# Batch 0 of an attention and two-MLP kernel with unscaled P, fp32 blocks of P^T stationary, V with a column of ones moving, and its first 256 queries in a stream of their own

## The chip, the cores and the metric

The kernel runs on one core of a Trainium2 chip. The metric is device time in microseconds. TensorE (PE) multiplies, and its weight loads are a row of their own (PEld); VectorE is DVE, ScalarE is ACT, GpSimd is POOL, and SyncE (SP) issues nearly all DMAs. A lower time is better.

## The reference

Attention over 4 batches, 8 heads, 576 positions and head size 64, with a causal mask and a decay bias from the running sum of the positive part of `s`; then an MLP with softplus, then an MLP whose activation is a rational function, both 512 to 2048 to 512 on 2304 tokens:

```python
scores = scale * q @ k.T                      # scale = 1/8
cum = np.cumsum(np.maximum(s, 0.0), axis=-1)
bias = -(cum[:, :, :, None] - cum[:, :, None, :])
scores = np.where(causal, -1e9, scores + np.minimum(bias, 0.0))
attn = np.exp(scores - scores.max(-1, keepdims=True))
attn = attn / (attn.sum(-1, keepdims=True) + 1e-09)
x = (attn @ v).transpose(0, 2, 1, 3).reshape(2304, 512)
h = x @ w_in;  x = (np.maximum(h, 0) + np.log1p(np.exp(-np.abs(h)))) @ w_out
h = x @ w_in2
g = (a0 + a1*h + a2*h**2 + a3*h**3) / (1 + abs(b0)*abs(h) + abs(b1)*h**2 + 1e-6)
out = g @ w_out2
```

The weights arrive as 64-bit floats and are converted on the chip.

## The kernel before

**Split operands.** Most products use the type fp32r. To keep precision, an operand is split into a rounded part (hi) and the rest (lo), and three products hi*hi, hi*lo, lo*hi are summed. The split of a tile is a copy on ACT (hi) and a subtraction on DVE or POOL (lo). In attention, `ht` and `st` hold both parts of q and k; four extra rows of `st` hold the running sum of `s` and ones, so that the scores' product (`scores`, two matmuls) adds the bias too.

**Attention parts.** A head of a batch is cut into parts of query rows: M (queries 0 to 255), B (256 to 383), H (384 to 575), L (M and B together). A part goes through `s1`/`s2` (scores on PE, mask with row minimum on DVE, Exp with row sum on ACT, `1/(sum+1e-9)` in two small DVE instructions, and the scaling of P by it on POOL, line 315), `t1`/`t2` (transposes of P on PE; `evac_pt` copies them out as hi on ACT, line 362, and lo on DVE, line 363), and `pv` (line 418: V stationary, hi and lo side by side in 128 columns; the hi and lo of P^T moving, 256 columns or more each, so that a product holds the V-hi half and the V-lo half in different partitions; a copy on ACT, line 429, and an addition on DVE, line 430, bring the halves together). The result goes into `x_t[b]`, with the model dimension in the partitions, as the first MLP wants it.

**Batch 0's start.** The first eight parts are the M parts of batch 0's heads. They have inputs of their own (`qk0`, `s0`), split by `prep_hi` and `prep_lo` (lines 232 to 238); `make_cum0` makes the running sum of their 256 positions. `make_cum` (lines 189 to 199) makes it for all heads and writes it to `cum_d` in DRAM, from where every later part loads its rows (line 275). Then come a B and an H part for each of the 8 heads, then the parts of batches 1 to 3.

**MLP.** Tokens are tiled as 256, 256 and four times 448 in the first MLP, and six times 384 in the second. A unit is one tile and one block of 128 of the 2048 hidden columns: `stage_a` (lines 670 to 672: 12 products), three elementwise stages, and `stage_b` (lines 706 to 708: 12 products). Units 0 to 7 are tile 0 with the blocks 0 to 7, units 8 to 15 tile 1 with the same blocks, units 16 to 31 both tiles in turn with the blocks 8 to 15; then come the 448-token tiles. Before a block is used, its weights are loaded and converted (`conv1`: line 536 on POOL, 537 on ACT, 538 and 543 on DVE, 547 on ACT, 548 on POOL, for each of the two halves of a block), and the lo part is written to `l_d` in DRAM (line 557).

**What sets the order.** Parts, conversions and units are recorded in one program; a list scheduler, with priorities by `ahead(...)`, then sets the order on each engine, which is fixed before the kernel runs. `stream` is the list of the steps of all parts, software pipelined (step `s1` of one part beside `t1`, `t2` of the part before it and `pv` of the one before that). Its first stretch, up to `marks[0]`, runs with the first 8 conversions ahead of the MLP; behind it, `gap` runs a share of the stream in each unit: the B and H parts of batch 0 within units 0 to 7, the L parts of batch 1 within units 8 to 31. SP issues its DMAs in order: one that waits for data holds up all behind it.

## Time and profile before

| | |
|---|---|
| time, median of 3 runs | 1103.66 us (1101.42 to 1104.06) |
| span of the profiled execution | 1100.2 us |
| PE, PEld busy | 94%, 84% |
| DVE, ACT, POOL busy | 75%, 76%, 44% |
| DMA | 140.53 MB, mean 128 GB/s |

The page gives the profiled execution as its span, from its first instruction to its last; no device time of that same execution stands beside it, so the runs' median serves, 3.5 us above it. Matmuls overlap, and the page models their ends, so the work of PE is better read from start to start of neighbouring matmuls than from its busy share. The words granted clock stand for the share of full speed that the throttle granted.

### The profile page before, as it was taken

Reading aid. Unit: us, or ns where it says so; the run is one execution under the profiler, and the core shown is the slowest. Engines: PE = TensorE matmul, PEld = TensorE weight load, DVE = VectorE, ACT = ScalarE, POOL = GpSimd, SP = SyncE. Lnnn points to the kernel's source line nnn. Section 1 sums busy time; section 2 is a strip of 40 time slices with the busy share of each in tenths; the row PEclk is TensorE's granted clock in tenths of the full one; section 3 lists DMA queues with packets and bytes.
Section 4 is the critical chain, followed back from the end, with each engine's and each line's share of the span. In section 5 each row is a group of like instructions: output and inputs, shape, how many; then the busy total and the mean of one; then the engine's idle time right before and its main releaser. Section 6 shows DMA issues by size and latency. Waiting matters only on the chain.

```text
span 1100.2 us, 17835 instructions
## 1 busy us (share of the span) xinstructions
PE 1030.3 (94%) x5732; PEld 926.5 (84%) x5732; DVE 825.4 (75%) x1904; ACT 836.6 (76%) x1767; POOL 488.2 (44%) x543
## 2 busy tenths in 40 slices
PE   3588889889999999999999999899999999999998
PEld 3477778789888888888999998799999999999996
DVE  6898998777888788886556677667777677776765
ACT  6698888878787788777556555688788888888885
POOL 3655576552222122221244676445445455454543
PEclk9999999999999999999999999899999999999999
DMA  6464566466555464432777974401000010000000
GB/s 227 167 221 158 181 222 217 162 205 178 166 160 158 142 205 132 154 94 66 226 235 223 323 280 149 160 1 45 13 30 29 1 58 1 29 30 1 30 1 29
DMA packets 70493, 140.53 MB, mean 128 GB/s; under 512 B 8384, under 2 KB 23904, under 8 KB 70400
## 3 DMA queue, kind: packets, MB, share of 16 engines
q1 hardware_dynamic: 68000, 135.37, 37.5%
q10 hardware_dynamic: 2400, 4.03, 1.5%
q8 instruction: 45, 0.74, 0.3%
q14 instruction: 48, 0.39, 0.1%
HBM read 112.66 MB, written 22.61 MB: 123 GB/s over the span
## 4 chain that ended last, share of the span: by engine, by line
PE 65%; DVE 5%; DMA 3%; ACT 3%; POOL 2%; issue 2%; SPq 0%; POOLq 0%; ACTq 0%; DVEq 0%
PE h L672 6%; PE h L671 6%; PE h L670 6%; PE acc L715 6%; PE acc L714 6%; PE acc L713 6%; PE at L418 3%; PE at L670 3%; PE at L672 3%; PE at L671 3%; PE acc L706 3%; PE acc L707 3%; PE acc L708 3%; PE at L318 2%; DMA raw64x<-in_w_dram 2%
## 5 line engine op out<-in xcount | busy, mean ns | idle before, releaser
L671 PE MATMUL h<-xs,w1h 128*128 128x448 f32 (+1 forms) x352 | 119.9, 341 | 1.4 <-DVE xs L640 1.4
L670 PE MATMUL h<-xs,w1h 128*128 128x448 f32 (+1 forms) x352 | 119.9, 342 | 1.3 <-DVE e L764 1.0
L707 PE MATMUL acc<-gl,w1h 128*128 128x448 f32 (+1 forms) x352 | 119.1, 338 | 1.2 <-POOL gl L802 1.2
L706 PE MATMUL acc<-gh,w1h 128*128 128x448 f32 (+1 forms) x352 | 119.7, 341 | 0.1
L672 PE MATMUL h<-xs,w1l 128*128 128x448 f32 (+1 forms) x352 | 118.8, 338 | 0.2 <-POOL w1l L548 0.2
L708 PE MATMUL acc<-gh,w1l 128*128 128x448 f32 (+1 forms) x352 | 118.4, 336 | 0.0
L715 PE MATMUL acc<-w2h,gl 128*128 128x512 f32 x288 | 113.8, 395 | 0.4 <-POOL gl L802 0.4
L713 PE MATMUL acc<-w2h,gh 128*128 128x512 f32 x288 | 113.8, 395 | 0.4 <-ACT gh L800 0.4
L714 PE MATMUL acc<-w2l,gh 128*128 128x512 f32 x288 | 113.6, 394 | 0.0
L315 POOL TENSOR_SCALAR PA<-PA,stat 128x384 f32<-128x384 f32 (+3 forms) x112 | 69.3, 622 | 97.2 <-DVE stat L314 51.9
L802 POOL TENSOR_TENSOR gl<-PA,gh 128x384 fp32r<-128x384 f32 x96 | 99.4, 1036 | 6.3 <-issue 4.0
L773 POOL TENSOR_TENSOR tc<-tc,e 128x384 f32<-128x384 f32 x48 | 51.7, 1076 | 102.7 <-ACT tc L771 102.7
L315 POOL TENSOR_SCALAR P<-P,stat 128x576 f32<-128x576 f32 x32 | 26.2, 819 | 143.2 <-DVE stat L313 50.7
L363 DVE TENSOR_TENSOR ptl<-at,pth 128x384 fp32r<-128x384 f32 (+2 forms) x108 | 60.7, 569 | 16.3 <-ACT pth L362 15.1
L312 ACT ACTIVATE PA<-PA,stat 128x384 f32<-128x384 f32 (+3 forms) x112 | 63.9, 571 | 10.3 <-DVE stat L299 9.0
L670 PEld LDWEIGHTS h<-xs,w1h 128*128 128x128 f32 x352 | 67.0, 191 | 5.5 <-DVE e L764 1.7
L671 PEld LDWEIGHTS h<-xs,w1h 128*128 128x128 f32 x352 | 66.8, 190 | 5.0 <-DVE xs L640 2.2
L707 PEld LDWEIGHTS acc<-gl,w1h 128*128 128x128 f32 x352 | 66.4, 189 | 4.9 <-POOL gl L802 2.0
L362 ACT ACTIVATE pth<-at 128x384 fp32r<-128x384 f32 (+2 forms) x108 | 53.3, 499 | 21.4 <-PE at L392 12.2
L706 PEld LDWEIGHTS acc<-gh,w1h 128*128 128x128 f32 x352 | 66.4, 189 | 3.6 <-DVE yb L736 0.5
L672 PEld LDWEIGHTS h<-xs,w1l 128*128 128x128 f32 x352 | 66.6, 189 | 3.1 <-POOL w1l L548 0.4
L708 PEld LDWEIGHTS acc<-gh,w1l 128*128 128x128 f32 x352 | 66.2, 188 | 3.0
(225 smaller groups left out, 3311.9 us busy)
## 6 DMA issues: line engine op xcount, KB each, us to landing
w1l<-l_d SPq DMA_DIRECT2D x148, 256.0 KB
raw<-in_w_dram SPq DMA_DIRECT2D x48, 512.0 KB
raw<-in_qk_dram SPq DMA_DIRECT2D x32, 384.0 KB
l_d<-w1l SPq DMA_DIRECT2D x32, 256.0 KB
raw64x<-in_w_dram SPq DMA_DIRECT2D x16, 512.0 KB
R<-in_vv_dram SPq DMA_DIRECT2D x16, 320.0 KB
raw<-in_qk_dram SPq DMA_DIRECT2D x8, 576.0 KB
out_dram<-yb SPq DMA_DIRECT2D x18, 256.0 KB
```

What stands on the lines that cost most here:

```text
L312: nc.scalar.activation(pt[:, 0:n], pt[:, 0:n], AF.Exp, bias=mn, scale=-1.0, accum_out=stat[:, i, 1:2])
L315: nc.gpsimd.tensor_scalar(pt[:, 0:n], pt[:, 0:n], stat[:, i, 2:3], 1.0, op0=ALU.mult, op1=ALU.mult)
L670: nc.tensor.matmul(h, wh[:, cs], xh, start=(k == 0), stop=False)
L671: nc.tensor.matmul(h, wh[:, cs], xl, start=False, stop=False)
L672: nc.tensor.matmul(h, wl[:, cs], xh, start=False, stop=(k == KD - 1))
L706: nc.tensor.matmul(o, wh[:, cs], gh, start=first and not both, stop=False)
L707: nc.tensor.matmul(o, wh[:, cs], gl, start=False, stop=False)
L708: nc.tensor.matmul(o, wl[:, cs], gh, start=False, stop=last and (not both or m % 2 == 1))
L713: nc.tensor.matmul(acc[m], gh[:, cs], wh, start=first, stop=False)
L714: nc.tensor.matmul(acc[m], gh[:, cs], wl, start=False, stop=False)
L715: nc.tensor.matmul(acc[m], gl[:, cs], wh, start=False, stop=last)
L802: eng.tensor_tensor(gl, g, f(gh), op=ALU.subtract)
```

## The change

For batch 0 alone (`turned`), and nothing else in the attention:

- P is not scaled. The Exp has no row sum, and the two small instructions and POOL's scaling go. V has a column of ones between the two heads of a pair (129 columns, input `vt`), so the product with V gives the row sums as a 65th column.
- In `pv_turned`, blocks of P^T (128 keys x 128 queries, plain fp32) are stationary and 65 columns of V move. P^T is copied out once, without a split: on ACT in `t1`, on DVE in `t2`. V isn't split. The output has queries in the partitions: one DVE pair for the reciprocal of each part's sums and a multiplication into `x_t[0]`, now laid out with 128 queries in the partitions.
- Batch 0's rows of x must then be transposed for the MLP: in `split_x_` PE transposes them into PSUM, and the split reads from there.
- The scores of the M parts are one plain fp32 product of 66 rows; the first block of queries takes 128 keys instead of 256. `prep_hi`, `prep_lo` and the splits of the running sum go. `qk0` is loaded with 64 partitions instead of 128.
- The eight M parts are a stream of their own, `steps(0, N0)`, drained before the B and H parts start; `turn0` splits tile 0's x in it, after each pair of heads. In it, the 8 conversions start after a third of its steps instead of half, `make_cum` is placed at that third instead of ahead of the stream, and the conversions' temporary comes from the larger pool `xs`. `load_raw` is now called in that stream too, for six M parts and three pairs of V, whose tiles nothing reads.

Places in the diff:

```diff
+        if p.turned:
+            nc.scalar.activation(pt[:, 0:n], pt[:, 0:n], AF.Exp, bias=mn, scale=-1.0)
+            return
         nc.scalar.activation(pt[:, 0:n], pt[:, 0:n], AF.Exp, bias=mn, scale=-1.0, accum_out=stat[:, i, 1:2])
...
     def scores(o, p, q0, k0, n):
+        if p.first:
+            nc.tensor.matmul(o, p.ht[:, 0, q0:q0 + 128], p.ht[:, 1, k0:k0 + n], start=True, stop=True)
+            return
...
+            n = 128 if p.first else 256
+            scores(bk[:, 0:n], p, 0, 0, n)
+            scores(bk[:, n:n + 256], p, 128, 0, 256)
...
+        if p.turned:
+            c0 = 0 if n == 3 else 320
+            nc.scalar.activation(p.pt[:, c0:c0 + n * 128], bk[:, 0:n * 128], AF.Copy)
...
+            if p.turned:
+                nc.vector.tensor_copy(p.pt[:, 384:768], bk[:, 0:384])
...
+        if p.turned:
+            nc.vector.tensor_copy(p.pt[:, 0:320], bk[:, 64:384])
...
+    def pv_turned(p):
+        bk = abank()
+        hd = p.h % 2
+        lo = [[(0, 0)], [(0, 128), (1, 256)]]
+        hi = [[(c, 384 + c * 128) for c in range(3)]]
+        far = [[(c, 320 + c * 128) for c in range(4)], [(c, c * 64) for c in range(5)]]
+        q0, blocks = {"M": (0, lo), "L": (0, lo + hi), "B": (2, hi), "H": (3, far)}[p.kind]
+        nb = len(blocks)
+        w = D + 1
+        for j, ops in enumerate(blocks):
+            for i, (c, o) in enumerate(ops):
+                nc.tensor.matmul(
+                    bk[:, j * w:(j + 1) * w], p.pt[:, o:o + 128], p.vs[:, c, hd * D:hd * D + w],
+                    start=(i == 0), stop=(i == len(ops) - 1))
...
+        nc.vector.tensor_scalar(rs[:, :, 1:2], o[:, :, D - hd * D:D - hd * D + 1], 1.0e-9, None, op0=ALU.add)
+        nc.vector.reciprocal(rs[:, :, 2:3], rs[:, :, 1:2])
+        for j0, j1, qb, m in ((0, 1, 3, 128), (1, 2, 0, 64)) if p.kind == "H" else ((0, nb, q0, 128),):
+            nc.vector.tensor_tensor(
+                x_t[p.b][0:m, qb:qb + j1 - j0, p.h * D:(p.h + 1) * D], o[0:m, j0:j1, hd:hd + D],
+                rs[0:m, j0:j1, 2:3].broadcast_to([m, j1 - j0, D]), op=ALU.mult)
...
+    steps(0, N0)
+    marks.append(len(stream))
+    steps(N0, NP_)
...
-        n_c = n_st - n_st // S_START
+        n_c = n_st // 3
...
+            if n == n_c:
+                load_raw(allp[N0])
+                load_raw(allp[N0 + 1])
+                with ahead(P_CUM):
+                    make_cum()
...
+                src = x_t[b][:, k, s0:s0 + w] if b else abank()[:, 0:w]
+                if b == 0:
+                    for q in range(0, w, 128):
+                        m = min(128, w - q)
+                        nc.tensor.transpose(
+                            src[:, q:q + m], x_t[b][0:m, (s0 + q) // 128 % 4, k * 128:(k + 1) * 128], ident[0:m, 0:m])
```

How the order moves, at three places. First PE at its very start. Before, the scores of the first head pair, and the head of PE's order, are pairs of a product on `ht` (128 rows) and one on `st` (68 rows):

```order
L318 MATMUL acc<-ht_135 128x256
L318 MATMUL h<-ht_135 128x256
L319 MATMUL acc<-st_136 128x256
L318 MATMUL acc<-ht_135 128x256
L319 MATMUL acc<-st_136 128x256
L319 MATMUL h<-st_136 128x256
L318 MATMUL h<-ht_135 128x256
L319 MATMUL h<-st_136 128x256
```

Now each query block is one product on the raw tile, the transposes (line 367) follow the fourth, and the products with P^T stationary (line 414) come next:

```order
L300 MATMUL acc<-raw_129 128x128
L300 MATMUL acc<-raw_129 128x256
L300 MATMUL h<-raw_129 128x128
L300 MATMUL h<-raw_129 128x256
L367 MATMUL acc<-ident,gh 128x128 x3
L300 MATMUL at<-raw_131 128x128
L300 MATMUL at<-raw_131 128x256
L367 MATMUL h<-ident,gh 128x128
L414 MATMUL acc<-v_133,pt 128x65 x3
```

Four products of 256 columns for a head became two, of 128 and 256 columns.

Second, DVE around one B and H pair in the stretch of units 0 to 7. Before (lines 313 and 314 are the row sums' reciprocal, 363 the lo parts, 430 the addition, 299, 305 and 308 the masks, 282 and 283 the split of q and k):

```order
L305 ISA P_747,stat<-acc,mask 128x288
L305 ISA stat 128x1
L283 TENSOR_TENSOR ht<-raw,ht 64x576
L313 TENSOR_SCALAR stat<-stat 128x1
L430 TENSOR_TENSOR x_277<-acc,tmp 64x192
L314 RECIPROCAL stat<-stat 128x1
L363 TENSOR_TENSOR ptl<-at,pth 128x384
L308 ISA P_747,stat<-at,mask,stat 128x288
L308 ISA stat 128x1
```

Now (421, 422 and 424 are the reciprocal and the multiplication of `pv_turned`, 386 and 394 the copies of P^T):

```order
L283 ISA P_748,stat<-at,mask 128x288
L283 ISA stat 128x1
L422 RECIPROCAL stat<-stat 128x2
L386 COPY pt<-acc 128x384
L424 TENSOR_TENSOR x_220<-at,stat 128x64
L424 TENSOR_TENSOR x_220<-at,stat 64x64
L286 ISA P_748,stat<-acc,mask,stat 128x288
L286 ISA stat 128x1
L421 TENSOR_SCALAR stat<-at 128x1
```

The reciprocals no longer stand between Exp and the transposes, and the subtraction of the 512-column P^T (line 363) has no successor here: ACT copies that tile alone.

Third, SP's queue around the write of `cum_d`. Before, four weight halves (line 521) are issued ahead of it (line 199), and two of V for later pairs (line 259):

```order
L521 DMA raw_199<-in_w_dram 128x1024
L521 DMA raw_201<-in_w_dram 128x1024
L259 DMA R<-in_vv_dram 128x640 x2
L521 DMA raw_395<-in_w_dram 128x1024
L521 DMA raw_397<-in_w_dram 128x1024
L253 DMA raw<-in_qk_dram 128x896
L199 DMA cum_d<-rows 128x1152
L521 DMA raw_440<-in_w_dram 128x1024
```

Now two halves (line 561) stand ahead of it (line 194), then loads that nothing reads (line 221 with 256 columns, line 228 with 258), and the third and fourth halves stand behind it:

```order
L561 DMA raw_171<-in_w_dram 128x1024
L221 DMA raw<-in_qk_dram 128x2x256
L228 DMA vr<-in_vt_dram 128x258
L221 DMA raw<-in_qk_dram 128x2x256 x2
L228 DMA vr<-in_vt_dram 128x258
L221 DMA raw<-in_qk_dram 128x2x256
L221 DMA raw<-in_qk_dram 128x896
L228 DMA vr<-in_vt_dram 128x645
L194 DMA cum_d<-rows 128x1152
L561 DMA raw_276<-in_w_dram 128x1024
L561 DMA raw_278<-in_w_dram 128x1024
```

Two weight halves moved behind the wait for the running sum, and six loads without a reader stand ahead of it.

## Rows read from the trace of the kernel before

**Rows 1.** Busy time by stretch of the span (us, with instructions)
```profile
core 0: us, PE busy (x) PEld busy (x) DVE busy (x) ACT busy (x) POOL busy (x), PEclk, DMA share, GB/s
...
11.00:57.00 46.00, 25.52 (x96) 20.67 (x95) 36.16 (x115) 31.12 (x78) 26.89 (x34) 1.00 0.63 211
57.00:137.00 80.00, 67.38 (x471) 59.80 (x470) 72.62 (x210) 70.27 (x169) 43.50 (x51) 0.98 0.56 184
137.00:170.00 33.00, 29.02 (x222) 26.90 (x222) 30.89 (x79) 28.22 (x78) 23.05 (x28) 1.00 0.69 231
170.00:240.00 70.00, 59.86 (x471) 57.20 (x470) 53.94 (x131) 57.94 (x149) 45.32 (x53) 1.00 0.57 189
240.00:520.00 280.00, 276.80 (x1648) 243.72 (x1647) 224.43 (x701) 221.17 (x503) 63.52 (x97) 1.00 0.48 146
```
**Rows 2.** Timeline, up to the first mask: start, duration, instruction, idle before it
```profile
2.46 0.46 DVE L166 TENSOR_SCALAR cum<-s_t 32x256 f32<-32x256 f32 x1 [1.30 <-DMA s_t<-in_s_dram]
...
7.44 2.68 SPq L215 DMA_DIRECT2D st<-cumc  x4
...
9.55 0.55 PE L319 MATMUL acc<-st 68*128 68x256 f32 x1 [1.31 <-ACT st L233]
...
11.00 0.29 DVE L299 CUSTOM_DVE_ANT_0 gh<-acc,mask 128x128 f32<-128x128 f32 x1
```
**Rows 3.** DVE by line and shape, 0 to 57 us: busy, mean ns
```profile
L237 DVE TENSOR_TENSOR st<-raw,ht 64x512 fp32r<-64x512 f32 x4 | 3.1, 775 | 2.6 <-ACT ht L232 2.6
L363 DVE TENSOR_TENSOR ptl<-acc,pth 128x384 fp32r<-128x384 f32 x5 | 2.7, 549 | 0.6 <-ACT pth L362 0.5
L314 DVE RECIPROCAL stat<-stat 128x1 f32<-128x1 f32 x18 | 2.7, 156 | 0.1
L313 DVE TENSOR_SCALAR stat<-stat 128x1 f32<-128x1 f32 x18 | 2.6, 146 | 0.3
```
**Rows 4.** PE's timeline, 27 to 57 us
```profile
39.06 0.41 PE L318 MATMUL acc<-ht 128*128 128x256 f32 x1
39.27 0.41 PE L319 MATMUL acc<-st 68*128 68x256 f32 x1
...
48.41 0.66 PE L318 MATMUL at<-ht 128*128 128x384 f32 x1 [1.68 <-ACT raw L537]
...
55.17 0.41 PE L670 MATMUL h<-xs,w1h 128*128 128x256 f32 x1
```
**Rows 5.** SP's timeline, 0 to 75 us
```profile
30.51 0.33 SPq L199 DMA_DIRECT2D cum_d<-rows  x1
...
35.40 3.11 SPq L557 DMA_DIRECT2D l_d<-w1l  x2
...
39.07 0.31 SPq L275 DMA_DIRECT2D st<-cum_d  x1
```
**Rows 6.** DVE by line and shape, 57 to 137 us
```profile
L314 DVE RECIPROCAL stat<-stat 128x1 f32<-128x1 f32 x25 | 3.9, 155 | 0.2
...
L363 DVE TENSOR_TENSOR ptl<-acc,pth 128x512 fp32r<-128x512 f32 x5 | 3.4, 680 | 0.0
...
L291 DVE TENSOR_TENSOR vs<-R,vs 128x640 fp32r<-128x640 f32 x3 | 2.9, 959 | 0.0
```
**Rows 7.** PE's timeline, 57 to 70 us
```profile
64.95 0.77 PE L392 MATMUL at<-ident,P 128*128 128x128 f32 x5 [1.27 <-POOL P L315]
65.47 0.48 PE L318 MATMUL at<-ht 128*128 128x512 f32 x1
...
66.49 0.77 PE L418 MATMUL acc<-pth,vs 128*128 128x256 f32 x5
67.09 0.76 PE L418 MATMUL acc<-ptl,vs 128*128 128x256 f32 x5
```
**Rows 8.** Waits, 57 to 137 us: total, times, longest
```profile
PEld at L392 <- POOL P L315: 5.3, 5, 1.6
```
**Rows 9.** ACT by line and shape, 57 to 137 us
```profile
L312 ACT ACTIVATION_READ_ACCUMULATOR PA<-PA,stat 128x1 f32 x17 | 3.2, 189 | 0.0
```

More of the change, by code (lines that the diff above doesn't have):

```diff
@@ L118, in moe_chain_kernel, with __init__ @@
     class Part:
[L119 removed]
+        def __init__(self, b, h, kind, rng, first, turned):
             self.b, self.h, self.kind, self.rng = b, h, kind, rng
[L121 removed]
+            self.fresh, self.first, self.turned = rng is not None, first, turned
     def cols(t, rng):
@@ L365, in t1 @@
     def t1(p):
-        p.ph, p.pl = pt_h[p.idx % 2], pt_l[p.idx % 2]
+        if p.turned:
+            p.pt = t_j("pt", [128, 1024], F32)
+        else:
+            if not pt_h:
+                for i in range(2):
+                    for lst, nm in ((pt_h, "pth"), (pt_l, "ptl")):
+                        t = t_j(nm, [128, 1024], F32R)
+                        nc.gpsimd.memset(f(t[:, 0:192]), 0.0)
+                        lst.append(t)
+            p.ph, p.pl = pt_h[p.idx % 2], pt_l[p.idx % 2]
         if p.kind == "B":
@@ L369, in t1 @@
         bk = abank()
-        if p.kind in "LM":
-            for i, c0 in enumerate((256, 0, 128)):
-                nc.tensor.transpose(bk[:, i * 128:(i + 1) * 128], p.p1[:, c0:c0 + 128], ident)
+        n = 3 if p.kind in "LM" else 4
+        order = (256, 0, 128) if n == 3 and not p.turned else range(0, n * 128, 128)
+        for i, c0 in enumerate(order):
+            nc.tensor.transpose(bk[:, i * 128:(i + 1) * 128], p.p1[:, c0:c0 + 128], ident)
+        if p.turned:
+            c0 = 0 if n == 3 else 320
+            nc.scalar.activation(p.pt[:, c0:c0 + n * 128], bk[:, 0:n * 128], AF.Copy)
+        elif n == 3:
             evac_pt([t[:, 192:576] for t in (p.ph, p.pl)], bk[:, 0:384])
         else:
-            for c in range(4):
-                nc.tensor.transpose(bk[:, c * 128:(c + 1) * 128], p.p1[:, c * 128:(c + 1) * 128], ident)
             evac_pt(
@@ L463, in moe_chain_kernel, with steps, at, turn0 @@
         ends.append(n)
-    for i in range(NP_ + 2):
-        def at(j):
-            return allp[j] if 0 <= j < NP_ else None
-        a0, a1, a2 = at(i), at(i - 1), at(i - 2)
-        nx, nx2 = at(i + (2 if i < 6 else 1)), at(i + 2)
-        if i == 6:
-            nx = None
-        if nx2 is not None and 8 <= i + 2:
-            stream.append((load_raw, nx2))
-        if a0 is not None:
-            stream.append((s1, a0))
-        if a2 is not None:
-            stream.append((pv, a2))
-        if i - 1 in ends:
-            marks.append(len(stream))
-        if nx is not None:
-            stream.append((prep, nx))
-        if a1 is not None:
-            stream.append((t1, a1))
-            stream.append((t2, a1))
-        if a0 is not None:
-            stream.append((s2, a0))
+    def steps(lo, hi):
+        for i in range(lo, hi + 2):
+            def at(j):
+                return allp[j] if lo <= j < hi else None
+            a0, a1, a2, nx, nx2 = at(i), at(i - 1), at(i - 2), at(i + 1), at(i + 2)
+            if nx2 is not None:
+                stream.append((load_raw, nx2))
+            if a0 is not None:
+                stream.append((s1, a0))
+            if a2 is not None:
+                stream.append((pv, a2))
+                if a2.first and a2.h % 2 == 1:
+                    stream.append((turn0, a2))
+            if i - 1 in ends[1:]:
+                marks.append(len(stream))
+            if nx is not None:
+                stream.append((prep, nx))
+            if a1 is not None:
+                stream.append((t1, a1))
+                stream.append((t2, a1))
+            if a0 is not None:
+                stream.append((s2, a0))
+    def turn0(p):
+        split_x(0, 0, p.h // 2)
+    steps(0, N0)
+    marks.append(len(stream))
+    steps(N0, NP_)
     pos = [0]
@@ L531, in conv_t @@
         hw = r[:, :, 1]
-        t = sb.tile([128, 512], F32, tag="tc", bufs=2, name="tc")
+        lead = m == 0 and region[0] == 0 and not units_open
+        t = t_xs([128, 512], F32) if lead else sb.tile([128, 512], F32, tag="tc", bufs=2, name="tc")
         ti = t.bitcast(I32)
```

205 lines of the change are left out of this document (91 added, 114 removed).

## The prediction, made before the result was known

> **What bounds the kernel now.** I read the stretches of the span first [rows 1]. From 240 us on PE is busy 276.8 of 280 us, and the batches and tiles worked there are not touched by the change; what moves the end is therefore when the kernel gets to that point. From 57 to 137 us, the stretch in which units 0 to 7 run beside the eight B and H pairs of batch 0, DVE is busy 72.6 of 80 us, ACT 70.3 and PE 67.4. PE's share flatters it: in work from start to start it is less. Five transposes of P take 0.52 us, so 0.104 each, and five products of 256 columns with V take 0.60, so 0.12 each [rows 7]. A unit has 24 products of 256 columns, eight units 192, or 23 us; a head's pair has 12 transposes (1.25), scores with 2944 columns in all (1.4 at the same rate) and 16 products with V (1.9), or 4.55, and eight of them 36. That is 59 of 80 us, so DVE sets this stretch. From 11 to 57 us nothing is full: DVE 36.2 of 46 us, PE 25.5 [rows 1], and PE runs at its lower level: two products of 256 columns start 0.21 us apart at 39 us [rows 4] against 0.12 later, which is 1.2 against 2.4 GHz, although the granted clock reads 1.00. The start is a chain: the input of the running sum is used at 2.46 us, its rows go out by DMA at 7.44, the product that needs them starts at 9.55, the first mask at 11.00 [rows 2]. The first unit starts at 55.17, the first scores of a B part at 48.41 [rows 4].
>
> **Term 1, the first mask: 4 us earlier.** Between 2.46 and 7.44 stand six DVE and two ACT instructions, and ACT is split between them and `prep_hi`. Three in a row are left, at about 0.46 us each by the first [rows 2], with their handovers 1.8 us: the DMA goes out at 4.3 us, lands 2.1 later as before, and the first mask starts at about 7.0.
>
> **Term 2, DVE's work.** Up to 57 us the change takes away: the splits of q and k for two pairs after 11 us (four instructions at 0.78, 3.1 us), the lo parts of P^T of eight M parts (8 x 0.55 = 4.4), eight of sixteen reciprocal pairs (8 x 0.30 = 2.4) [rows 3], and two splits of V (at 0.96 each, 1.9 [rows 6]); 11.8 us. From 57 to 137 us: the lo parts of eight 512-column P^T, which ACT now copies alone (8 x 0.68 = 5.4), four splits of V (3.8), and 8 of 24 reciprocal pairs (2.4) [rows 6]; 11.6 us. The copies of 384 and 320 columns take the place of subtractions of the same size, and three multiplications of 64 columns a pair that of two additions: I count them at nothing, with 1 us either way. From 11 to 137 us DVE is busy 108.8 of 126 us, 86% [rows 1]. Without 23.4 us of it, at that share, the two stretches take 99 us instead of 126: 27 us less, and with term 1 the ceiling is 31 us.
>
> **Term 3, what SP's order gives back: 6 us.** A B part needs its rows from `cum_d`. Their load stands in SP's queue behind four writes to `l_d`, of which two wait for the third and fourth weight halves, whose loads now stand behind the write of `cum_d`; that write waits for `make_cum`. The scan now stands behind five heads' masks on DVE. A head needs about 3 us of PE at the lower level (term 4), so it begins at 22 us, and I put the write at 29 us, against 30.51 now [rows 5]. From the write to the load it takes 8.6 us now (30.51 to 39.07, with the two writes to `l_d` held up till 35.40 [rows 5]); a load and conversion more, some 7 us, and the first scores of a B part come at about 45 us, only 3 us earlier than now. Behind the load wait, on SP, the weight halves that follow. Until 45 us DVE has eight M parts (about 1.6 us each by the masks, the pair and the multiplication), the running sum, five or six halves, tile 0's split and one part's split of q and k: some 27 us of the 33 that it would do at 86%. The 6 us are lost, between 0 (if the parts aren't late) and 14 (if the fourth half is one more round late). The loads without a reader are covered by the free half of the DMA time there [rows 1]; if they aren't, it is in that 14. The first unit itself, which needs the M parts and one half, starts at about 37 us.
>
> **Term 4, PE's price for plain fp32: 4 us.** The trace shows plain fp32 only as transposes: 128 columns and a load of a 128x128 fp32 tile, 0.104 us [rows 7]. A product with V now loads such a tile and moves 65 columns. Lower end: a transpose, 0.10. Upper end: four, 0.42. I take 0.20, by the nearest row, the transpose, doubled because a product must carry the digits that a transpose passes through. A pair then has 12 such products, 2.4 us instead of 1.9; PE's work in the stretch becomes 63 us of the 67 that DVE would need, and two engines that full wait for each other: 4 us. At 0.10 it is 53 us and nothing is lost. For the M parts, at the lower level: scores 384 columns, between 0.32 us (the rate of [rows 4]) and four times that; with the upper end, 0.5 for transposes and 3 x 0.4, a head takes 3.0 us, eight heads 24, and the stream ends near 35 us with its last chain. The 20 new transposes of x cost 2 us of PE where it waits anyway.
>
> The Trainium skill bears on this price. FP8 and Floating Point Precision, TensorE Precision Notes, gives true FP32 four passes through the array, and TensorE: Matmul & The Clock Gate, Terms, calls the transpose mode four times faster for FP32. By these the price is the upper end, 0.42, if each pass loads its tile, and about a product of 260 columns, 0.12, if the loads hide; no row here shows which. The first makes rival B.
>
> **Covers.** POOL's scaling goes for batch 0. It held PE five times, 5.3 us in all [rows 8], but off DVE's path, which is late next; I count nothing. ACT loses 25 reads of row sums (0.19 each [rows 9]) and most copies, and is not late. From 137 to 240 us nothing is removed; I pass the gain on whole.
>
> **Sum.** 31 - 6 - 4 = 21 us. The span goes from 1100.2 to 1079; the runs' median lies 3.5 us above the span, so 1103.66 - 21 gives 1083 us. About 0.3%, 3.3 us, is what a measurement of this kernel can tell from no change.
>
> **Rivals.**
>
> A, the forecast, 1083 (1073 to 1092): 58%.
>
> B, PE takes over. At 0.42 us a pair costs PE 7.7 us with transposes and scores, the stretch 23 + 61 = 84 us: no gain there. The M stream takes 4.3 us a head, 34 us, and the B parts start no earlier; of the ceiling 13 us of the second stretch and 11 of the first are gone: 31 - 24 = 7, 1097 us. For it: the rule above. Against it: the products of a group share nothing that must be loaded four times, and the transpose pair already includes its load. 12%.
>
> C, the gain is given back before 240 us. From 170 to 240 us sixteen units take 70 us for 46 us of PE work, and no engine is full (PE 59.9, ACT 57.9 [rows 1]): the conversions run as a chain through POOL, ACT and DVE. If they set their own pace from the start, through SP's order, half of the 21 us is lost there: 1093. Against it: the halves are placed by units, and start earlier with them. 13%.
>
> D, slower. The same place as B at a higher price: at 0.55 us the stretch has 23 + 8 x 9.25 = 97 us of PE work, 17 more than it takes now, and the M stream 5.1 us a head, 41 us, so the first unit starts at 54 and nothing is won ahead of it but some 4 us; 1103.66 + 13 gives 1117. It decides from about 0.47 us a product on. Against it: this is more than four transposes. 8%.
>
> E, more than the sum: terms 3 and 4 are nothing, and DVE's copies and multiplications are shorter than what they replace: 1070. 9%.
>
> **Range and chances.** 1068 to 1100 leaves out D, parts of B and the end of E, some 15%. Faster by more than 0.3% are A, E and most of B and C: 0.84; within 0.3% the upper part of B: 0.08; slower 0.08.
>
> **What would show it.** The first mask near 7 us; the write of `cum_d` near 29, the first scores of a B part near 45, the first unit near 37; the stretch of the eight pairs about 71 us instead of 80, with DVE's work about 11 us less; the distance from its end to the end of the span unchanged within 3 us. PV products 0.2 us apart at the higher level. The forecast is wrong if these products stand 0.4 us apart, if the write of `cum_d` or the third half comes later than now, or if the stretch from the last H part to the 448-token tiles grows.

## The result and the profile after

The changed kernel takes 1110.25 us (median of 4 runs, 1106.57 to 1113.17) against 1103.42: a ratio of 1.007, 95% interval 1.0045 to 1.0094. Run again beside the experiments it gave 1110.75, ratio 1.0063 (1.004 to 1.0085). It is slower, by 0.6 to 0.7%; forecast were 1083 us and a gain of 21. Its two traces are of runs of 1106.57 and 1106.05 us, so a trace of it shows less than it lost: the span is 1104.8 us, 4.6 longer than before (1104.2 in the second trace), where the medians lie 7 to 9 us apart. A run's time is 1.8 us above its own span (1106.57 and 1104.8); the rest of the 3.5 us between median and span before is the distance of the traced run from the median.

Busy time by stretch of the changed kernel, columns as in [rows 1]:
```profile
core 0: us, PE busy (x) PEld busy (x) DVE busy (x) ACT busy (x) POOL busy (x), PEclk, DMA share, GB/s
...
11.00:57.00 46.00, 33.19 (x129) 27.99 (x128) 25.64 (x75) 21.60 (x45) 13.14 (x14) 1.00 0.61 196
57.00:137.00 80.00, 72.48 (x516) 67.45 (x516) 61.80 (x192) 57.77 (x111) 30.43 (x35) 0.97 0.63 203
137.00:170.00 33.00, 30.76 (x238) 29.61 (x237) 29.17 (x82) 29.22 (x80) 23.75 (x27) 0.97 0.67 221
170.00:240.00 70.00, 59.50 (x447) 57.27 (x446) 52.29 (x130) 56.05 (x141) 45.53 (x52) 0.95 0.58 189
240.00:520.00 280.00, 277.31 (x1666) 244.35 (x1666) 223.46 (x696) 221.07 (x504) 66.94 (x99) 1.00 0.49 146
```
DVE lost the work that was to go: 36.2 to 25.6 us from 11 to 57, 72.6 to 61.8 from 57 to 137. PE took its place as the fullest engine: 25.5 to 33.2 and 67.4 to 72.5. From 170 to 240 us the granted clock is 0.95, where before it was 1.00.

The start, against [rows 2, 4]; the first mask, and one M head on PE:
```profile
4.65 2.61 SPq L204 DMA_DIRECT2D raw<-cumc  x4
...
8.67 1.62 PE L300 MATMUL acc<-raw 66*128 66x128 f32 x4 [8.67 <-DMA raw<-cumc]
...
10.45 0.29 DVE L277 CUSTOM_DVE_ANT_0 gh<-acc,mask 128x128 f32<-128x128 f32 x1 [6.60 <-PE acc L300]
```
```profile
12.17 1.49 PE L300 MATMUL at<-raw 66*128 66x128 f32 x4
13.45 0.42 PE L367 MATMUL h<-ident,gh 128*128 128x128 f32 x1
13.66 1.38 PE L414 MATMUL acc<-v,pt 128*128 128x65 f32 x6
14.84 0.74 PE L300 MATMUL acc<-raw 66*128 66x128 f32 x2
```
A head's plain fp32 scores take 1.28 us (12.17 to 13.45), its three products with V 1.18 (13.66 to 14.84). Each plain fp32 product is two instructions, so "x6" is three products. PE is at its lower level here: a transpose takes 0.21 us (13.45 to 13.66), against 0.104 at the higher [rows 7].

SP of the changed kernel, against [rows 5]; L194 writes `cum_d`, L249 loads rows of it, L221 loads q and k, L561 a weight half, L599 writes a low half:
```profile
35.32 0.33 SPq L194 DMA_DIRECT2D cum_d<-rows  x1
35.70 1.38 SPq L561 DMA_DIRECT2D raw<-in_w_dram  x2
...
50.12 2.00 SPq L599 DMA_DIRECT2D l_d<-w1l  x2
52.22 0.38 SPq L561 DMA_DIRECT2D raw<-in_w_dram  x1
52.65 0.34 SPq L249 DMA_DIRECT2D st<-cum_d  x1
...
65.45 2.87 SPq L599 DMA_DIRECT2D l_d<-w1l  x2
68.36 0.43 SPq L221 DMA_DIRECT2D raw<-in_qk_dram  x1
...
69.33 0.34 SPq L249 DMA_DIRECT2D st<-cum_d  x1
```
The write of `cum_d` comes 4.8 us later than before, the first load of its rows 13.6 later, and the second head's q and k wait until 68.36 behind the writes of low halves.

What this does to PE, against [rows 4, 7]:
```profile
42.59 0.41 PE L718 MATMUL h<-xs,w1h 128*128 128x256 f32 x1
...
56.28 0.66 PE L302 MATMUL acc<-ht 128*128 128x384 f32 x1 [4.03 <-DVE ht L257]
...
77.44 2.12 PE L414 MATMUL acc<-vr,pt 128*128 128x65 f32 x18
79.37 0.38 PE L302 MATMUL acc<-ht 128*128 128x288 f32 x1
...
80.07 0.49 PE L384 MATMUL at<-ident,PA 128*128 128x128 f32 x3
```
The first unit starts 12.6 us earlier, the first B scores 7.9 later, the second head's B transposes at 80.07 (68.3 before). At the higher level nine products with V take 1.93 us, 0.21 each.

**The stations of each trace.** Second head: its B transposes; eighth head: its H transposes; unit 32 is the first on 448 tokens. changed_again is the changed kernel unedited, in a second trace. Times in us; the time and ratio are of all runs. The kernel before was run again beside each group of experiments, with medians from 1101.9 to 1103.1 us, so kernels of different groups are compared by their ratios.

| kernel | second head | eighth head | unit 8 | unit 16 | 16 to 32 | 32 to end | time | ratio (interval) |
|---|---|---|---|---|---|---|---|---|
| before | 68.3 | 134.7 | 130.4 | 170.1 | 70.8 | 859.3 | 1103.4 | |
| changed | 80.1 | 129.7 | 137.2 | 170.4 | 74.3 | 860.1 | 1110.3 | 1.007 (1.0045-1.0094) |
| changed_again | 80.0 | 129.7 | 134.9 | 168.6 | 75.7 | 860.0 | 1110.8 | 1.0063 (1.004-1.0085) |
| late_v | 78.5 | 131.6 | 136.7 | 168.9 | 72.2 | 860.4 | 1102.2 | 0.9986 (0.9971-1.0001) |
| second_head | 72.9 | 126.0 | 132.3 | 166.3 | 72.5 | 860.2 | 1100.4 | 0.9985 (0.9968-1.0002) |
| half_first | 79.2 | 128.9 | 136.2 | 169.5 | 73.4 | 860.6 | 1106.7 | 1.0037 (1.0025-1.0049) |
| few_pv | 78.9 | 128.1 | 131.5 | 166.0 | 72.8 | 863.5 | 1098.2 | 0.9969 (0.9953-0.9985) |
| start_order | 75.5 | 124.7 | 129.9 | 163.0 | 75.8 | 863.3 | 1105.3 | 1.0028 (1.0015-1.004) |
| own_stream_all | 66.2 | 130.8 | 135.3 | 169.4 | 74.7 | 860.2 | 1104.5 | 1.0006 (0.9979-1.0034) |
| own_stream_loads | 64.5 | 125.1 | 127.2 | 162.9 | 71.2 | 861.6 | 1099.0 | 0.9974 (0.9959-0.9988) |
| one_stream | 70.0 | 122.8 | 127.9 | 160.5 | 75.1 | 861.7 | 1098.5 | 0.9963 (0.9948-0.9978) |
| sum_first | 69.7 | 122.5 | 127.7 | 160.2 | 74.7 | 860.6 | 1098.2 | 0.9968 (0.9956-0.998) |
| sum_first_few | 69.4 | 119.5 | 121.8 | 157.5 | 71.1 | 862.6 | 1093.9 | 0.9928 (0.9903-0.9952) |
| sum_first_m | 65.2 | 117.9 | 123.1 | 155.7 | 75.4 | 860.2 | 1093.8 | 0.992 (0.9901-0.994) |
| sum_first_split | 69.9 | 123.7 | 124.2 | 160.5 | 74.7 | 861.1 | 1097.8 | 0.9952 (0.9936-0.9969) |
| sum_first_u0 | 67.2 | 118.9 | 124.1 | 157.8 | 76.3 | 862.8 | 1098.0 | 0.9972 (0.9954-0.999) |
| u0_half_first | 67.3 | 119.1 | 124.3 | 158.1 | 72.1 | 862.1 | 1096.1 | 0.9953 (0.9934-0.9972) |
| u0_and_split | 67.2 | 120.1 | 120.6 | 156.6 | 71.7 | 862.9 | 1093.1 | 0.9913 (0.9893-0.9933) |

From before to changed: the second head comes 11.8 us later, the heads after it follow faster (from the second's B transposes to the eighth's 60.4 us before, 43.5 after), and at unit 16 the two stand level. The forecast had 21 us there. Of the 4.6 us lost in the trace, 3.5 come from units 16 to 32. The two traces of the changed kernel differ by 2.3 us at unit 8, 1.8 at unit 16 and 1.4 over units 16 to 32, so such a difference between two traces shows nothing by itself. The column from unit 32 to the end differs by up to 4 us between kernels whose instructions are the same there, so a span alone decides nothing below that. Runs of one kernel can lie apart too, own_stream_all's the most: four took 1098.0 to 1099.1 us at a mean granted clock of 0.992 to 0.995, six 1102.9 to 1109.2 us at 0.975 to 0.986, and its trace is one of the six.

### The profile page after: what moved, and what is told of

Same layout as the page of the kernel before. It is cut to its first block, busy times and chain, and to the rows that moved or that the text cites. A ratio compares the mean times of both kernels' runs of the same rounds, so it can differ in the third digit from the quotient of the medians.

```text
span 1104.8 us, 17814 instructions
## 1 busy us (share of the span) xinstructions
PE 1048.8 (95%) x5832; PEld 948.6 (86%) x5832; DVE 795.4 (72%) x1847; ACT 812.3 (74%) x1672; POOL 463.5 (42%) x504
## 4 chain that ended last, share of the span: by engine, by line
PE 68%; DVE 9%; DMA 6%; issue 6%; ACT 5%; POOL 5%; SPq 1%; POOLq 0%; ACTq 0%; DVEq 0%
PE h L718 6%; PE h L719 6%; PE h L720 6%; PE acc L768 6%; PE acc L767 6%; PE acc L766 6%; PE at L449 3%; PE at L720 3%; PE at L718 3%; PE at L719 3%; PE acc L759 3%; PE acc L760 3%; PE acc L761 3%; DMA raw64x<-in_w_dram 3%; PE at L302 2%
## 5 line engine op out<-in xcount | busy, mean ns | idle before, releaser
L718 PE MATMUL h<-xs,w1h 128*128 128x448 f32 (+1 forms) x352 | 122.7, 349 | 5.4 <-ACT xs L687 2.9
L719 PE MATMUL h<-xs,w1h 128*128 128x448 f32 (+1 forms) x352 | 122.4, 348 | 1.0 <-DVE xs L688 1.0
L720 PE MATMUL h<-xs,w1l 128*128 128x448 f32 (+1 forms) x352 | 121.5, 345 | 1.1 <-POOL w1l L589 1.1
L759 PE MATMUL acc<-gh,w1h 128*128 128x448 f32 (+1 forms) x352 | 120.6, 343 | 0.1
L296 POOL TENSOR_SCALAR PA<-PA,stat 128x128 f32<-128x128 f32 (+3 forms) x96 | 59.1, 618 | 84.4 <-DVE stat L295 46.2
L718 PEld LDWEIGHTS h<-xs,w1h 128*128 128x128 f32 x352 | 69.1, 197 | 10.3 <-DVE e L817 3.5
L296 POOL TENSOR_SCALAR P<-P,stat 128x576 f32<-128x576 f32 x24 | 20.4, 849 | 130.6 <-DVE stat L294 54.5
L719 PEld LDWEIGHTS h<-xs,w1h 128*128 128x128 f32 x352 | 69.4, 197 | 4.6 <-DVE xs L688 1.6
L720 PEld LDWEIGHTS h<-xs,w1l 128*128 128x128 f32 x352 | 69.1, 196 | 4.5 <-POOL w1l L589 1.6
L760 PEld LDWEIGHTS acc<-gl,w1h 128*128 128x128 f32 x352 | 67.2, 191 | 2.9
L768 PEld LDWEIGHTS acc<-w2h,gl 128*128 128x128 f32 x288 | 54.3, 189 | 13.4 <-POOL gl L855 0.8
L348 DVE TENSOR_TENSOR ptl<-at,pth 128x384 fp32r<-128x384 f32 (+1 forms) x95 | 53.6, 571 | 16.6 <-ACT pth L347 15.2
L767 PEld LDWEIGHTS acc<-w2l,gh 128*128 128x128 f32 x288 | 54.3, 188 | 12.2
```

What stands on the lines that cost most here:

```text
L296: nc.gpsimd.tensor_scalar(pt[:, 0:n], pt[:, 0:n], stat[:, i, 2:3], 1.0, op0=ALU.mult, op1=ALU.mult)
L348: nc.vector.tensor_tensor(l, src, f(h), op=ALU.subtract)
L718: nc.tensor.matmul(h, wh[:, cs], xh, start=(k == 0), stop=False)
L719: nc.tensor.matmul(h, wh[:, cs], xl, start=False, stop=False)
L720: nc.tensor.matmul(h, wl[:, cs], xh, start=False, stop=(k == KD - 1))
L759: nc.tensor.matmul(o, wh[:, cs], gh, start=first and not both, stop=False)
```

## Experiments: the start

Theory S: the order of SP's queue makes the heads late. Theory P: PE is the bound once the heads run. Theory G: what is won by 137 us is given back by 240.

**late_v.** Batch 1's V loads wait for the write of `cum_d`:
```
# make_cum, behind its DMA
+        cum_t["w"] = traced()[-1]
# load_raw, behind the load of R from vv
+                    queue_behind({cum_t["w"].engine: cum_t["w"]}, k0)
```


> The changed kernel, with one edit: the loads of batch 1's first two V tiles, which the changed kernel issues at about 3 us ahead of the rows of the running sum, are held behind the write of cum_d. Theory S (the order of SP's queue at the start costs the time): the rows land about 2 us after their issue instead of 4, the first mask starts near 8.3 us instead of 10.45, and the M stream and the write of cum_d come 2 us earlier; of that at most 2 us reach the end, 1108. Theory P (from 80 us PE is the bound with the turned heads) and theory G (whatever is won ahead of 137 us is given back by 240 us) both say that the end does not move: 1110 within 2 us.

The rows went out at 4.18 and the first product started at 7.85: landing still took 3.7 us, the mask came only 0.8 us earlier. The time fell by 8 us all the same, of which the trace shows 1.5 at unit 16 and 2.1 behind it, where the edit touches nothing. At unit 16 the second trace of the changed kernel is as early as late_v's (168.6 and 168.9). The stretch behind it is taken up below.

**second_head.** The second head's loads stand in the start:
```
-                load_raw(allp[N0 + 1])
+                load_raw(allp[N0 + 2])
...
             prep(allp[N0])
+            prep(allp[N0 + 2])
```


> The changed kernel with one edit: the loads of q, k and of the rows of the running sum for the second head's B and H parts are issued in the start, beside the first head's, instead of behind the eight halves that are converted there. Theory S (the heads from the second on take 7 us each whatever they wait for, so the time at which the second begins sets the end of the stretch): its B transposes at 70 us instead of 80.1, the eighth head's H transposes near 121 instead of 129.7, unit 8 near 129 instead of 137.2, the end 5 to 8 us below the changed kernel's. Theory P (PE is the bound): units 4 and 5, which now run in the gap, are pushed behind the heads, the eighth head comes at 127 or later and the end moves by less than 2 us.

This took 10.4 us less than the changed kernel run beside it (1100.38 to 1110.75; between the ratios lie 0.8%, some 9 us). SP of second_head, L251 loading the rows of two heads:
```profile
47.23 0.55 SPq L221 DMA_DIRECT2D raw<-in_qk_dram  x1
53.20 0.68 SPq L251 DMA_DIRECT2D st<-cum_d  x2
```
The second head came at 72.9, the eighth at 126.0, unit 8 4.9 us earlier, although the write of `cum_d` left 3.5 us later than in the changed kernel (38.79). S holds in sign; but unit 4 moved from 72.4 to 83.1, as P said. The trace has 4.1 us of the gain at unit 16 and 1.7 in units 16 to 32 (2.3 and 3.1 against the second trace of the changed kernel); where the rest arises isn't shown.

**start_order.** The sum ahead of the stream, four halves ahead of it, loads without a reader left out, V late:
```
+        with ahead(P_CUM):
+            make_cum()
         for n in range(n_st):
...
-        load1_to(2)
+        load1_to(4)
...
-        if p.fresh:
+        if p.fresh and not p.first:
```


> The changed kernel with four edits, all of them to what stands on SP and ahead of the first unit: the running sum is emitted ahead of the M stream, four weight halves are loaded ahead of it instead of two, the loads that no one reads (q, k and V of the M parts) are left out, and batch 1's V loads wait for the write of cum_d. Theory S: the write of cum_d at 28 us (35.3 in the changed kernel), the first scores of a B part at 46 us (56.3), the second head's B transposes at 70 us (80.1), the end 10 us earlier: 1100. Theory P: the heads from 80 us on take 7 us each on PE as before, so half of it at most is kept: 1105. Theory G: the unit of tile 1 that opens the next stretch still starts near 137 us, the end at 1109.

It took 1105.3 us, short of S. The write of `cum_d` left at 41.8, not 28: the planner had put it behind two writes of low halves.

**own_stream_all.** start_order, with low halves behind the write, `P_CUM = 400`, and the loads of second_head:

> The changed kernel, with its stream of M parts of its own, and all of the start's edits together: the loads that no one reads left out, batch 1's V loads and the writes of low halves behind the write of cum_d, four weight halves ahead of it, the running sum emitted first with its priority raised from 60 to 400, and the loads for two heads (not one) in the start. Theory S: the write of cum_d at 33 us, the first scores of a B part at 45, the second head's B transposes at 58 to 62, the first unit at 36; the eighth head's H transposes 60 us after the second head's start, 119, unit 8 at 122, the end 1090 to 1093. Theory P (from the second head on PE is full, so units that ran in the gap before are pushed behind): unit 8 at 127 as in sum_first and the end at 1098.

It missed both theories: 1104.5 us, unit 8 at 135.3. The write of `cum_d` left at 40.1, not 33. The second head came at 66.2, the third only at 86.2. SP, with L605 the write of low halves and L222 the third head's q and k:
```profile
69.27 2.90 SPq L605 DMA_DIRECT2D l_d<-w1l  x2
72.28 0.77 SPq L222 DMA_DIRECT2D raw<-in_qk_dram  x1
```
The wait had moved one head on.

**own_stream_loads.** All batch-0 heads' loads ahead:
```
-            with ahead(off):
+            with ahead(400 if fn in (load_raw, prep) and g == 1 else off):
```


> own_stream_all with one more edit: the loads and the preparation of every B and H part of batch 0 have the priority 400, so that on SP the loads of the third to sixth head stand among the first eight writes of low halves and not behind them. Theory S (what the own stream loses is the order of the later heads' loads on SP): third head's B transposes at 73 to 76 us instead of 86.2, the following heads 7 us apart, unit 8 at 125, the end 1092 to 1096. Theory P (PE is the bound from the second head on, whichever work it gets): the heads come earlier and the units 4 to 7 as much later, unit 8 at 130 or later, the end 1100 or more.

The third head came at 74.6, unit 8 at 127.2, between S and P, and unit 16 6.6 us earlier than in own_stream_all: in the traces the later heads' place on SP was the own stream's loss. The time is less sure: 1099.0 us, by the ratios 3.5 us less with intervals that overlap, and four of own_stream_all's runs lie as low.

**one_stream.** The changed arithmetic with the order of before:
```
-    steps(0, N0)
-    marks.append(len(stream))
-    steps(N0, NP_)
+    steps(0, NP_)
```
with the sum, weight halves and gate at the start as in the kernel before (`P_CUM = -100`), and the loads of start_order.

> The changed kernel with its batch-0 arithmetic (plain fp32, turned products) but with the order of the kernel before: one stream for M, B and H parts, the running sum ahead of it, the prepared B parts inside the start, weight halves as in the kernel before; the loads that no one reads are left out and batch 1's V loads wait for the write of cum_d. Theory S: the first scores of a B part at 46 us or earlier, two heads ready together, units 0 to 7 end some 10 us earlier than in the kernel before, and the end is 1092. Theory P: the end stays at 1106 or above since the turned heads cost PE more than they save DVE. Theory G: 1103, as the kernel before.

It took 1098.5 us: the new arithmetic in the old order, without the loads that nothing reads and with batch 1's V loads held back as in late_v, is a gain of 4 us. The changed kernel lies 12 us above it, 9.9 of them at unit 16; that is what its order costs, with those loads. The busy time of one_stream:
```profile
57.00:137.00 80.00, 76.41 (x596) 72.72 (x595) 68.03 (x210) 62.89 (x132) 32.63 (x40) 0.97 0.64 208
```
PE is busy 76.4 of 80 us, DVE 68.0: with the heads in time PE, not DVE, is the fullest engine. What its work there is worth is tested next.

## Experiments: PE's price

**few_pv**, on the changed kernel, and **sum_first_few**, on sum_first:
```
+            if p.kind != "M":
+                ops = ops[0:1]
```


> The changed kernel, but the products of P^T with V of batch 0's B and H parts are cut to the first key block of each: 3 products a head pair instead of 12 (its result is that of a part of the keys only). At the 0.21 us of the trace that takes 1.9 us a head, 15 us in all, from PE and nothing from any other engine. Theory P: most of it, 8 to 12 us, shows at the end: 1100. Theory S: heads start as late as before and only their own chain gets shorter, 3 us: 1107. Theory G: no change, 1110.

> sum_first, with the products of P^T with V of batch 0's B and H parts cut to the first key block of each: 3 instead of 12 for a head pair (its result is that of a part of the keys only), which takes 15 us of work from PE. Theory P: with two heads loaded in time PE is the bound from 57 to 131 us (it is busy 76 of 80 us in the neighbouring kernel one_stream), so unit 8 starts 10 us or more earlier, near 117, and the end falls by 8 or more to 1090. Theory S (each head's own chain of loads, split, scores, mask and exponent takes 7 us, and PE's share of it is small): unit 8 moves by 3 us at most, the end by 3, 1095.

Both leave out most of the products, so their results are not the attention's. few_pv gave 12 us (10 to 11 by the ratios), but its heads still come 7.3 us apart and its traced span is only 2.5 us shorter; the trace is of a run of 1104.12 us, with a granted clock of 0.84 from 57 to 137 us. sum_first_few gave 4.3. Its unit 8 came 5.8 us earlier, between P's 10 and S's 3, and its unit 16 2.8; another 3.6 come in units 16 to 32, where the order on SP changed too, which the next part takes up. So 15 us of PE's work are worth 3 to 6 where the heads are in time, and heads 7.4 us apart instead of 7.9 say that PE is not all that sets them. What else does isn't shown.

**sum_first**, one_stream with
```
         nc.sync.dma_start(out=l_d[ff][half], in_=f(l))
+        queue_behind({cum_t["w"].engine: cum_t["w"]}, k0)
```


> one_stream with one more edit: no write of a low half to l_d stands ahead of the write of cum_d on SP. In one_stream the rows were ready at 34 us and the write left at 38.6, behind two such writes. Theory S: the write leaves at 34, the first load of its rows at 41 or 42 instead of 46.6 and the first scores of a B part 4 us earlier, unit 8 near 124 instead of 127.9, the end 2 to 4 us below one_stream's: 1095. Theory G (half or more of what is won by 130 us is lost by 240 us): 1097. If the weight chain and not the rows paces the start of the heads: no change, 1098.5.

Nothing changed, the third of the cases put down: the write left at 33.9, 4.7 us earlier, and the first B transposes stayed at 56.5. The rows' load didn't move with the write, since it still stands behind writes of low halves and a weight half: it left at 46.66, and at 46.65 in one_stream.

**sum_first_m**, M parts without their off-diagonal block:
```
-            scores(bk[:, n:n + 256], p, 128, 0, 256)
+            scores(bk[:, n + d:n + 256], p, 128, d, 256 - d)   # d = 128 for M
```


> sum_first, with the M parts cut to their two diagonal blocks (queries 128 to 255 don't see keys 0 to 127): 256 instead of 384 columns of plain fp32 scores, two transposes instead of three, two products with V instead of three, which at the lower level is 0.43 + 0.2 + 0.39 us a head, 8 us of PE in all, and 0.1 us a head each of DVE and ACT. If PE's plain fp32 products pace the start (DVE and ACT sat waiting for PE from 10 to 30 us): the running sum's scan 3 us and the last M part's products 6 to 8 us earlier, the first scores of a B part and unit 0 some 4 us earlier, the end 2 to 4 us lower, 1095. If the loads and the conversion of the first weight halves pace it: the M parts end earlier but unit 0 and unit 8 don't move, 1098.

The excerpt is one of several places; queries 128 to 255 leave out keys 0 to 127. Unit 0 came at 53.8 (59.0), unit 16 4.6 us earlier, the end 4.4: of the edits to sum_first this one arrived in full. The M parts' work paces the start, and nearly all that was taken is PE's plain fp32 at the lower level (DVE and ACT lost 0.1 us a head); 1 us of PE a head is worth over 4 us of the end.

**sum_first_split** (tile 1's x turned back per pair) and **sum_first_u0** (unit 0 ahead of the first B work):
```
+SP1B = (5, 3, 2, 1)      # for T = 1, in place of SP1
```
```
+                if i == N0:
+                    stream.append((pv, a1))
+                    stream.append((turn0, a1))
```


> sum_first with one more edit: x of tile 1 is turned back and split for a pair of heads as soon as the pair is done (5, 3, 2 and 1 units ahead of unit 8 instead of 2, 1, 1 and 1), where one_stream had six of its eight transposes between 127.6 and 130.9 us. Theory S adds: if those transposes and splits at the end of the stretch hold unit 8, it starts 2 to 4 us earlier and the end is 2 us lower still, 1093; if the last head's own products hold it, no change against sum_first, or 1 us more since the splits now stand among the heads' work.

> sum_first with one more edit: the last M part's product with V and the turning of tile 0's last x stand ahead of the first B and H parts' scores on PE, not behind them; with that, unit 0 stands ahead of the first B part's transposes. In sum_first PE was busy 28.9 of 46 us from 11 to 57 and unit 0 began at 59.0, behind scores that wait for their rows. Theory P (PE's work up to unit 8 is the bound, so what is done in PE's idle time before 57 us is won): unit 0 at 47 to 50, unit 8 3 us earlier, 124.5, the end 1095. Theory S (the heads' own chain): the heads stay where they are, unit 8 at 127.5 and the end at 1098.

Each put unit 8 3.5 us earlier, and neither median moved by more than 0.4. For sum_first_split the lead was gone at unit 16; for sum_first_u0 it was 2.4 us there (157.8 to 160.2) and 0.8 at unit 32.

## Experiments: units 16 to 32

The table's column for units 16 to 32 has two groups: short, 70.8 to 73.4, and long, 74.3 to 76.3. Which one a kernel falls in goes with one place on SP. What stands there, changed kernel and late_v (numbers of buffers left out):
```
changed                          late_v
st<-cum_d                        st<-cum_d
raw<-in_qk   (waits for DVE)     raw<-in_w
raw<-in_w                        l_d<-w1l
raw<-in_w                        raw<-in_qk
```
All nine traces of the long group have the load of q and k ahead of both halves, as on the left; none of the others has. SP there, changed kernel (L249 rows, L221 q and k, L561 weight halves), then late_v (L252, L222, L564):
```profile
179.80 0.66 SPq L249 DMA_DIRECT2D st<-cum_d  x1
183.83 0.34 SPq L221 DMA_DIRECT2D raw<-in_qk_dram  x1
185.27 0.93 SPq L561 DMA_DIRECT2D raw<-in_w_dram  x2
```
```profile
176.37 0.67 SPq L252 DMA_DIRECT2D st<-cum_d  x1
179.31 0.34 SPq L564 DMA_DIRECT2D raw<-in_w_dram  x1
181.29 0.33 SPq L602 DMA_DIRECT2D l_d<-w1l  x1
183.23 0.34 SPq L222 DMA_DIRECT2D raw<-in_qk_dram  x1
```
What the load of q and k waits for in the changed kernel is DVE's split of an earlier q and k (L257, which ends at 183.75), and not PE, as the expectation of half_first has it; from 176 to 190 us:
```profile
SPq L221 <- DVE ht L257: 3.3, 1, 3.3
```
The half goes out 6.0 us later, 3.4 of which are there at the rows already. POOL's next conversion (L577, in late_v L580) starts 6.7 later:
```profile
191.50 0.64 POOL L577 TENSOR_SCALAR tc<-raw 128x512 f32<-128x512 f32 x1 [2.94 <-PE at L303]
```
```profile
184.83 0.64 POOL L580 TENSOR_SCALAR tc<-raw 128x512 f32<-128x512 f32 x1
```
No edit of late_v stands here: the planner lays the whole program out anew, and a DMA moved at 3 us turned this pair at 180.

**half_first** and **u0_half_first**: the changed kernel and sum_first_u0, with that pair turned and every order up to 170 us left alone:
```
+            if fn is load_raw and g == 2 and p.h == 0:
+                queue_behind({cum_t["lw"].engine: cum_t["lw"]}, k0)   # lw: the last weight half's load
```


> The changed kernel with one edit, which leaves every engine's order as it is up to 170 us: the load of q and k for batch 1's first H part, which waits on SP for PE at about 180 us, is put behind the two weight-half loads that stand right behind it. Theory O (this one order on SP costs the stretch of units 16 to 32 some 3 us, and the edits late_v, second_head and few_pv each owed a part of their gain to changing it): units 16 to 32 take 71 to 72.5 us instead of 74.3 and 75.7, the span is 3 us shorter, and the time 3 to 6 us, 1104 to 1107, a ratio of 1.001 to 1.004 to the kernel before. Theory S alone (the start is the whole loss): no change, 1110.5.

> sum_first_u0 with the same edit as half_first. Theory O: sum_first_u0 opened unit 8 3.6 us earlier than sum_first and ended no earlier, since its units 16 to 32 took 76.3 us; with the half's load first they take 71 to 73, and the end is at 1094 to 1095, near u0_and_split's 1093. Without it: 1098.

half_first took 3.9 us less than the changed kernel's 1110.5, in the range given, though the intervals of the ratios overlap a little. Units 16 to 32 did not do what was expected: they fell by 0.9 us only, within what two traces of one kernel differ by, since the halves still left at 184.3. u0_half_first fell by 1.9 us (intervals overlap), units 16 to 32 by 4.2.

A second thing differs, which no run holds fixed: the granted clock. From 170 to 240 us, for sum_first_u0, u0_half_first and half_first (the changed kernel's row stands above):
```profile
170.00:240.00 70.00, 59.80 (x432) 56.62 (x432) 52.01 (x118) 52.77 (x133) 41.67 (x46) 0.95 0.55 177
```
```profile
170.00:240.00 70.00, 60.86 (x458) 57.31 (x457) 53.35 (x130) 56.03 (x141) 45.22 (x47) 1.00 0.57 186
```
```profile
170.00:240.00 70.00, 58.49 (x458) 55.62 (x457) 51.37 (x128) 56.90 (x143) 45.57 (x52) 1.00 0.58 190
```
A mean of 0.95 over 70 us is at most 3.5 us of PE at full speed, an estimate from this row alone, and the changed kernel lost 3.5 us there against the kernel before at 1.00. The clock does not sort the groups by itself: u0_and_split is short at 0.95, sum_first long at 0.98. The order on SP sorts them, and twice less time went with turning it. That it is the cause is likely and not shown, and its 1 to 4 us are not told apart from the clock's.

**changed_again** is the changed kernel unedited, for the comparisons above.

> The changed kernel unedited, beside the runs that follow, on one chip with them. If the 8 us by which it lay above late_v come from the edit, it lies at 1107 to 1111 again, a ratio of 1.005 to 1.009 to the kernel before; if they come from the chip of that day, it lies at 1102 to 1104.

It took 1110.75 us, the first of the two cases put down: the 8 us to late_v were not the chip's.

**u0_and_split**, both edits on sum_first:

> sum_first_u0 with the early splits of tile 1 of sum_first_split: the version that the runs point to. Theory P: unit 8 opens at 121 to 122 us (124.1 in sum_first_u0; the splits gained 3.5 us there in sum_first_split). Theory G (the conversions, which stand with the units of both tiles in one order, pace the stretch from unit 8 to the 448-token tiles, so a lead at unit 8 alone is lost): unit 32 starts at 234 to 235 as in all four versions with one stream, and the end is at 1097 to 1098.5, a ratio of 0.995 to 0.997 to the kernel before. If the lead is passed on, 1094 to 1095.

It took 1093.1 us, ratio 0.9913 (0.9893 to 0.9933): faster than both kernels, and against Theory G the lead was passed on, with unit 32 at 228.3. It fell in the short group:
```profile
57.00:137.00 80.00, 75.66 (x607) 72.21 (x607) 68.60 (x220) 65.12 (x138) 34.75 (x41) 1.00 0.67 215
137.00:170.00 33.00, 30.77 (x246) 29.54 (x245) 26.83 (x74) 28.86 (x78) 23.68 (x29) 1.00 0.72 239
170.00:240.00 70.00, 63.62 (x459) 60.27 (x457) 52.03 (x127) 56.00 (x141) 40.71 (x47) 0.95 0.59 192
```
PE is busy 63.6 of 70 us from 170 to 240, against 59.5 in the changed kernel.

## Why the prediction was wrong

Two steps failed: the turning of DVE's work into time (term 2), by the most, and SP's order (term 3), which made the sign.

- **Term 1** (the first mask 4 us earlier): 0.55. The rows went out at 4.65 (I had 4.3) but landed after 4.0 us, not 2.1, and the mask came 1.8 us behind the landing, for which my 7.0 left 0.6 although [rows 2] show 1.45. The V loads ahead of the rows explain little: without them the landing took 3.7. What does stays open.
- **Term 2** (DVE's work, 11.8 and 11.6 us): the work was right, 10.5 and 10.8. Wrong was to turn it into 27 us of time by DVE's share. The ceiling less term 4 puts unit 16 27 us earlier; one_stream, the same arithmetic with the heads in time, has it 9.6 earlier than the kernel before, and u0_and_split, the best order that was run, 13.5. With DVE's work gone PE is the fullest engine. I had it at 63 of 67 us and took off 4 for that; from 11 to 137 us it is busy 105.7 of 126 us against DVE's 87.4, and in one_stream 76.4 of 80 us from 57 to 137. But PE alone is not the whole bound: 15 us less work on it brought unit 8 forward by 5.8 us. The heads, 10.1 us apart before, came 7.3 apart (60.4 and 43.5 us for six).
- **Term 3** (SP's order gives back 6 of 0 to 14 us): it cost 9.9, and on another path. I had the write of `cum_d` at 29 and the first B scores at 45; they came at 35.3 and 56.3. I followed one load through SP's queue and not the next head's: the second came 11.8 us later than before. Unit 16 comes 9.9 us later than in one_stream, inside the bounds of 0 to 14, and that uses up the 9.6 that one_stream gains. Putting that one head's loads ahead took some 9 to 10 us off the time, of which the traces show 2.3 to 4.1 at unit 16.
- **Term 4** (plain fp32): 0.20 us a product with V was right, 0.21 measured, and the M scores' upper end too, 1.28 us a head. But I let the start's PE work count only as the stream's end; sum_first_m shows it arriving in full. The Trainium skill's rule of four passes (FP8 and Floating Point Precision, TensorE Precision Notes) agrees with the scores, 384 columns in 1.28 us against 256 in 0.21 for the rounded type [rows 4]; the product of 65 columns lies between the two prices that I drew from it, 0.12 and 0.42.
- **The gain is passed on whole from 137 us**: wrong by 3.5 us in the trace, over units 16 to 32. It goes with an order on SP that I didn't compare, and with a granted clock of 0.95. The tail from unit 32 was unchanged within 1 us, as said.

Of the rivals, B had the engine and not the price (0.42 a product). C had the place and the kind (a weight half late through SP) with a gain left over. D had the sign but not the mechanism: it put it on the price of a product. Two of the signs of being wrong came: the write of `cum_d` was later than before, and the stretch from the last H part to the 448-token tiles grew from 106.2 to 115.0 us.

Not settled: the 3 to 7 us by which the changed kernel's other runs lie above its two traces; how much of late_v's 8 us is its own; and what besides PE sets the pace of the heads.

## What to carry to other kernels

On a queue that issues in order, follow every later user of it, not the first: a load that is moved back by one wait moves back all that stand behind it, and when one is pulled ahead the wait shows up at the next. Work taken off the busiest engine is worth no more than the distance to the next engine or to the chain that feeds it; compute that distance first. Where a planner lays out the program, an edit can reorder places far from it, so compare the order of the whole program and the time by stretch before an edit is given its gain.

## What the runs showed of the hardware

A plain fp32 product shows as two matmul instructions in the trace; of 65 columns it takes 0.21 us at the higher level of PE's clock and 0.39 at the lower. In the start the granted clock reads 1.00 ([rows 1], and the first rows behind the result), while products of 256 columns stand 0.21 us apart [rows 4], against 0.12 at the higher level. In one_stream it reads 0.76 from 11 to 57 us and in sum_first 1.00, and unit 0 starts at 58.98 and 58.99: in this case the reading alone does not tell which level PE runs at.
